# Turning h's columns between the halves of a product, and block 0's order and columns moved, in a routed expert stage

## The chip, the cores and the metric

One core of a Trainium2 chip runs the whole program. The metric is the device time of one execution in microseconds (us). The engines are PE (matrix products; PEld is its weight load, PEldq its sequencer in the rows), DVE, ACT, POOL and SP. DVE and ACT do the arithmetic between products, SP and POOL issue the transfers. Each engine works through its own queue in order, and waits on semaphores of others.

## The reference

Three stages follow each other on 1792 tokens (4 x 448) of 768 features:

```python
attn = 1.0 / (1.0 + np.exp(-(scale * q @ k.T - np.log(S))))    # 12 heads, sigmoid attention
x = attn @ v
do_compute = x @ w_skip > 0                # the other tokens pass unchanged
e_idx = np.argmax(x @ w_gate, axis=1)      # one of 8 experts for each token
y = gate_w * (np.maximum(x @ w1[e], 0.0) @ w2[e])      # w1: 768x1024, w2: 1024x768
x = x + y
g = elu(x @ w_in);  out = g @ w_out        # dense, 768 -> 2048 -> 768
```

All of it is in float32. The kernel makes each product out of three products of split operands (high x high, high x low, low x high), which keeps float32's accuracy.

## The kernel before, in words

**Stages.** Attention with the gate's logits runs until about 205 us of the profiled span, the expert stage until about 465 us, the dense layer to the end. The change is in the expert stage (lines 657 to 1144).

**Blocks.** The tokens that are computed are sorted by expert into blocks of up to 256 slots, two halves of 128 rows. A block has a kind, which PE and the other engines load into a register and branch on (`level`, L1106): SINGLE (first half alone), FEW (second half with at most 64 rows) or WHOLE. With these inputs block 0, 1 and 3 are WHOLE, 2 and 4 are FEW, 5, 6 and 7 are SINGLE, and then `close` (L1067) leads into the dense layer. A block that has two halves passes two branches, L1121 (`few`) and L1125 (`many`); the arm that isn't taken runs `rest` (L1100) instead, which is one tiny instruction on PE, ACT and DVE each. The branch hint ahead of them (`skips`, L1119; it shows as L1367 in the rows) tells PE's sequencer where the branch will go.

**One block.** `columns` (L773) turns the gathered rows into columns: four PE flips per group of features, three groups, into the PSUM tiles pt0, pt1 and acc1 (`ends`); for each group ACT copies the high part (L769) and DVE subtracts for the low part (L771). `hold_up` puts 14 filler products between the first flip of block 0 and the next. Then the products with w1 follow. In WHOLE blocks (`up_two`) h comes out with its features on partitions and needs no turning. In the others (`up_parts`) it comes out by rows; ACT copies it to SBUF (`hs`, L871; `hf`, L873), PE flips it (`h_columns`, L778: half 0 with flips at L138, the second half of a FEW block with L786) and ACT (L793) and DVE (L794) write its high and low columns. `h_columns(0)` turns the first half of h's features, `h_columns(1)` the second. Then `back` (L875) does the products with w2, chunks 4 to 7, each 4 steps of three products in 12 instructions per half (8 for a FEW half): chunks 4 and 5 take the first half of h's features, 6 and 7 the second. `outcome` (L923) adds gate times product into the rows (DVE, L931); for a FEW half ACT first copies y to SBUF (L881) and PE folds it (L930).

**What is left over.** Only chunk 4 of the first half is done inside a block's arm. Chunks 5 to 7 of it run inside the next block, behind that block's `columns` (`between`, L971, and `lead_in`, L985).

**Weights.** SP fetches chunks of 128x1536 into a ring of 13 (L710). For each, ACT casts the high part (L734) and DVE subtracts for the low part (L736), into a ring of 4. `ahead(i, c)` (L820) does that two chunks ahead of use; `ahead(i, 5)` (L902) is the last one in an arm, ahead of `h_columns(1)` on the queues of ACT and DVE.

**Block 0.** `lead_in` (L990) does its columns ahead of the two arms. In its arm the order of tokens and slots for the later gathers is worked out: DVE steps beside the products (`places_in_order`), 12 DVE compares (`order_rows`, L1043), and at the arm's end `slot_order` (L1047): 12 small products into acc1 and a chain of DVE instructions, L1054 to L1065, on which the gather of block 2 waits.

**Order.** PE, ACT and DVE run in the order in which the code is written.

Of the kernel before, what the change touches and what calls it, by code (L numbers as in the profile page):

```python
# [23 lines left out]
P = 128  # L24
# [10 lines left out]
KF1 = F1 // P  # L35
# [6 lines left out]
N2 = DM // 2  # L42
WCH = 1536
FA = 9
TB = 4
NOR = NTT // TB * TB
# [43 lines left out]
def build(nc, tc, a):  # L90
# [3 lines left out]
    with ExitStack() as top:  # L94
# [563 lines left out]
        with ExitStack() as st:  # L658
# [114 lines left out]
            def columns(i):  # L773
                for g in range(3):
                    flip_rows(i, g, ends[g])
                    split_columns(g, ends[g], x2)

            def h_columns(nh, sizes):  # L778
                for h, n in enumerate(sizes):
                    pt = pt_t[(nh + h) % 2].rearrange("p (c n) -> p c n", c=4)[:, :, :n]  # L780
                    for j in range(4):
                        w = slice(j * P, (j + 1) * P)
                        if n == P:
                            flip(pt[:, j, :], hs_t[nh][:, w])
                        else:
                            nc.tensor.matmul(  # L786
                                pt[:, j, :], hf_t[nh][:, w], fold[:, :n], start=True, stop=True
                            )
                    t = slice(h * P, h * P + n)
                    h_hi, h_lo = h2[:, nh, 0, :, t], h2[:, nh, 1, :, t]  # L790
                    if n < P:
                        h_lo = h2[:, nh, 0, :, h * P + n : (h + 1) * P]
                    nc.scalar.activation(h_hi, pt, AF.Relu)  # L793
                    nc.vector.scalar_tensor_tensor(  # L794
                        h_lo, pt, 0.0, h_hi, op0=ALU.max, op1=ALU.subtract
                    )
# [4 lines left out]
            def h_part(s, k):  # L801
                return h2[:, k // 4, s, k % 4]

            def product(o, h, n, a2, i, c, width, k0, total):

                t = slice(h * P, (h + 1) * P)
                for j in range(WCH // width):
                    w = slice(j * width, (j + 1) * width)
                    hi, lo = (u[:, w] for u in weights(i, c))
                    a_hi, a_lo = (a2(s, k0 + j)[:, t] for s in range(2))  # L810
# [61 lines left out]
                        else:  # L872
                            nc.scalar.copy(hf_t[nh], acc_t[(3, 0)[nh]])  # L873

            def back(i, h, n, chunks):  # L875

                for c in chunks:
                    c4, nh = divmod(c - 4, 2)
                    product(py[nh][h], h, n, h_part, i, c, N2, 4 * c4, KF1)
                    if n < P and c4:  # L880
                        nc.scalar.copy(yf_t[nh], py[nh][h])  # L881

            def expert(i, sizes, following=None):
# [5 lines left out]
                        outcome(i - 1, 0, P)  # L889

                if i == 0:
                    split_w(0, 1)
                if whole:
                    up_two(i, aside, soon)
# [8 lines left out]
                if i == 0:  # L903
                    run(aside)
                    order_rows()
                for h, n in list(enumerate(sizes))[1:]:
                    if whole:
                        back(i, h, n, range(4, 8))
                        outcome(i, h, n)
                        back(i, 0, P, range(4, 5))  # L910
                    else:
                        back(i, h, n, range(4, 6))
                        h_columns(1, sizes)
                        back(i, h, n, range(6, 8))
                        back(i, 0, P, range(4, 5))
                        outcome(i, h, n)
                if i == 0:
                    slot_order()
                if len(sizes) == 1:
                    back(i, 0, P, range(4, 5))  # L920
                    h_columns(1, sizes)

            def outcome(i, h, n):  # L923

# [60 lines left out]
            def lead_in(i):  # L985

                if i:
                    back(i - 1, 0, P, range(7, 8))
                else:
                    columns(0)  # L990

            def places_in_order():

# [52 lines left out]

            def slot_order():  # L1047

                og = acc_t[1][:, :NOR]
                for t in range(NOR):  # L1050
                    nc.tensor.matmul(
                        og, one_hot[:, t], ca[:, t], start=(t == 0), stop=(t == NOR - 1)
# [318 lines left out]
```

## Time and profile before

| | us |
|---|---|
| median of 3 timed runs | 950.01 |
| lowest and highest of them | 943.79 and 951.31 |
| the profiled execution | 946.63 |
| its span, first to last instruction | 944.9 |
| PE busy in the span | 907.7 (96%) |

In timeline rows the columns are start (us from the span's start), duration (us), engine, line, operation, output<-inputs, shape and count of merged instructions; the brackets give the engine's idle time just before and what ended it.

### The profile page before, as it was taken

Reading aid. Unit: us, or ns where it says so; the run is one execution under the profiler, and the core shown is the slowest. Engines: PE = TensorE matmul, PEld = TensorE weight load, DVE = VectorE, ACT = ScalarE, POOL = GpSimd, SP = SyncE. Lnnn points to the kernel's source line nnn. Section 1 sums busy time; section 2 is a strip of 40 time slices with the busy share of each in tenths; the row PEclk is TensorE's granted clock in tenths of the full one; section 3 lists DMA queues with packets and bytes.
Section 4 is the critical chain, followed back from the end, with each engine's and each line's share of the span. In section 5 each row is a group of like instructions: output and inputs, shape, how many; then the busy total and the mean of one; then the engine's idle time right before and its main releaser. Section 6 shows DMA issues by size and latency. Waiting matters only on the chain.

```text
span 944.9 us, 13400 instructions
## 1 busy us (share of the span) xinstructions
PE 907.7 (96%) x5047; PEld 738.9 (78%) x5047; DVE 585.7 (62%) x893; ACT 504.5 (53%) x703; POOL 71.2 (8%) x69
## 2 busy tenths in 40 slices
PE   7899999999999899999799999999999999999997
PEld 4555555549998898888688888888888888888997
DVE  4777877967756556688578888533443434434664
ACT  7777776535346336577354455444443444443664
POOL 0000000020220210233100000000000100000100
PEclk9999999999999999999999999999999999999999
DMA  9989897569962583594653333000010100000100
GB/s 247 266 234 272 250 270 246 170 228 404 379 250 84 217 325 115 196 410 185 226 197 101 106 106 107 34 34 1 17 34 18 51 17 1 1 0 1 68 1 34
DMA packets 33989, 139.46 MB, mean 148 GB/s; under 512 B 4874, under 2 KB 5514, under 8 KB 33890
## 3 DMA queue, kind: packets, MB, share of 16 engines
q1 hardware_dynamic: 29410, 119.17, 37.6%
q0 software_dynamic: 4480, 19.01, 5.6%
q8 instruction: 57, 0.93, 0.4%
q14 instruction: 42, 0.34, 0.1%
HBM read 117.58 MB, written 23.60 MB: 149 GB/s over the span
## 4 chain that ended last, share of the span: by engine, by line
PE 82%; DVE 3%; DMA 3%; issue 2%; ACT 2%; SPq 0%; ACTq 0%; DVEq 0%
PE acc L1246 15%; PE pt L1246 9%; PE acc L1213 8%; PE acc L1214 8%; PE acc L1215 8%; PE acc L743 6%; PE acc L745 6%; PE acc L744 6%; PE ps L239 3%; PE po L253 3%; DMA wo<-wo_d 1%; PE acc L815 1%; PE pt L138 1%; PE acc L816 1%; PE acc L138 1%
## 5 line engine op out<-in xcount | busy, mean ns | idle before, releaser
L736 DVE TENSOR_TENSOR wlo<-raw,whi 128x1536 fp32r<-128x1536 f32 x64 | 111.2, 1756 | 35.1 <-ACT whi L734 34.7
L1222 ACT ACTIVATE m<-acc 128x512 f32<-128x512 f32 (+1 forms) x64 | 34.9, 545 | 175.3 <-PE acc L1215 168.6
L1224 DVE SCALAR_TENSOR_TENSOR m<-m,acc 128x512 f32<-128x512 f32 (+1 forms) x64 | 39.7, 621 | 141.9 <-ACT m L1223 141.9
L734 ACT CAST whi<-raw 128x1536 fp32r<-128x1536 f32 x64 | 94.0, 1481 | 25.7 <-DMA raw<-in_w 6.7
L246 ACT ACTIVATE at<-ps,bias 112x896 f32<-112x896 f32 x96 | 89.1, 1008 | 30.4 <-PE ps L239 30.2
L1246 PE MATMUL acc<-wol,gh 128*128 128x256 f32 x320 | 101.0, 316 | 0.0
L1246 PE MATMUL acc<-woh,gl 128*128 128x256 f32 x320 | 100.5, 314 | 0.0
L1246 PE MATMUL acc<-woh,gh 128*128 128x256 f32 x320 | 100.4, 314 | 0.0
L1214 PE MATMUL acc<-x,wih 128*128 128x512 f32 (+1 forms) x270 | 96.0, 356 | 0.0
L1213 PE MATMUL acc<-x,wih 128*128 128x512 f32 (+1 forms) x270 | 95.9, 355 | 0.0
L1215 PE MATMUL acc<-x,wil 128*128 128x512 f32 (+1 forms) x270 | 95.6, 354 | 0.0
L743 PE MATMUL acc<-whi,both 128*128 128x384 f32 (+1 forms) x236 | 84.3, 357 | 0.6 <-PE acc L745 0.6
L744 PE MATMUL acc<-wlo,both 128*128 128x384 f32 (+1 forms) x236 | 83.0, 352 | 0.0
L745 PE MATMUL acc<-whi,both 128*128 128x384 f32 (+1 forms) x236 | 83.0, 352 | 0.0
L253 PE MATMUL po<-at,vt 112*64 112x448 f32 x384 | 77.5, 545 | 0.7 <-DVE xT L261 0.7
L1202 DVE TENSOR_TENSOR wol<-wo,woh 128x768 fp32r<-128x768 f32 x64 | 61.2, 956 | 23.4 <-ACT woh L1201 23.0
L1246 PEld LDWEIGHTS acc<-woh,gh 128*128 128x128 f32 x320 | 60.3, 188 | 10.1
L1246 PEld LDWEIGHTS acc<-wol,gh 128*128 128x128 f32 x320 | 60.3, 188 | 9.3
L1201 ACT CAST woh<-wo 128x768 fp32r<-128x768 f32 x64 | 53.4, 834 | 26.0 <-PE acc L1246 25.9
L1228 DVE TENSOR_TENSOR gl<-m,gh 128x512 fp32r<-128x512 f32 (+1 forms) x64 | 40.0, 626 | 40.5 <-ACT gh L1227 40.5
L1246 PEld LDWEIGHTS acc<-woh,gl 128*128 128x128 f32 x320 | 60.1, 188 | 4.3
L239 PE MATMUL ps<-qs,kh 128*112 128x448 f32 x192 | 58.1, 384 | 3.7 <-ACT at L246 2.2
(234 smaller groups left out, 1950.1 us busy)
## 6 DMA issues: line engine op xcount, KB each, us to landing
raw<-in_w SPq DMA_DIRECT2D x66, 768.0 KB
kr<-in_k SPq DMA_DIRECT2D x22, 448.0 KB
raw<-in_wi SPq DMA_DIRECT2D x9, 768.0 KB
raw<-in_wo SPq DMA_DIRECT2D x9, 768.0 KB
vt<-in_v SPq DMA_DIRECT2D x12, 448.0 KB
x_d<-xr SPq DMA_DIRECT2D x14, 384.0 KB
raw<-in_wi SPq DMA_DIRECT2D x14, 384.0 KB
raw<-in_wo SPq DMA_DIRECT2D x14, 384.0 KB
```

The source lines that it names most:

```text
L239: nc.tensor.matmul(ps[:CP, j, :S], kk[:, 2 * p + j, c * CP : (c + 1) * CP], qs[:, p, j], start=(i == 0), stop=(i == 1),)
L246: nc.scalar.activation(at[:, :, c, :], ps[:CP, :, :S], AF.Sigmoid, bias=bias[:CP], scale=QK_SCALE)
L253: nc.tensor.matmul(po[64 * j : 64 * j + 64, :S], vt[:, 2 * (hp % 2) + j, c, :], at[:, j, c, :], start=(c == 0), stop=(c == NCH - 1),)
L734: nc.scalar.copy(w_hi, raw)
L736: nc.vector.tensor_sub(w_lo, raw, w_hi)
L743: nc.tensor.matmul(o, a_hi, b_hi, start=first, stop=False)
L744: nc.tensor.matmul(o, a_hi, b_lo, start=False, stop=False)
L745: nc.tensor.matmul(o, a_lo, b_hi, start=False, stop=last)
L1213: nc.tensor.matmul(o, a, b, start=(cc == 0), stop=False)
L1214: nc.tensor.matmul(o, a, c, start=False, stop=False)
L1215: nc.tensor.matmul(o, wil[:, cc], b, start=False, stop=(cc == KD - 1))
L1246: nc.tensor.matmul(o, a, b, start=(clears and f == 0 and k_ == 0), stop=(f == KF2 - 1 and k_ == 2), skip_group_check=True,)
```

## The change

Four things change. `h_columns` does the second half (h = 1) first, then half 0. In a FEW arm `h_columns(1)` stands one chunk earlier, between chunks 4 and 5 of h = 1, and `outcome` stands between the two halves (two steps each) of chunk 4 of half 0. In a SINGLE arm `h_columns(1)` stands between those halves and not behind both. In block 0 `slot_order` runs ahead of chunk 4 of half 0 (for a WHOLE block) and writes acc0 instead of acc1, and block 0's `columns` stands in each arm's beginning, so behind the branches.

```diff
             def h_columns(nh, sizes):
-                for h, n in enumerate(sizes):
+                for h, n in reversed(list(enumerate(sizes))):
...
-            def product(o, h, n, a2, i, c, width, k0, total):
+            def product(o, h, n, a2, i, c, width, k0, total, part=slice(None)):
...
-                for j in range(WCH // width):
+                for j in range(WCH // width)[part]:
...
-            def back(i, h, n, chunks):
+            def back(i, h, n, chunks, part=slice(None)):
...
-                    product(py[nh][h], h, n, h_part, i, c, N2, 4 * c4, KF1)
+                    product(py[nh][h], h, n, h_part, i, c, N2, 4 * c4, KF1, part)
...
                 if i == 0:
+                    columns(0)
                     split_w(0, 1)
...
-                for h, n in list(enumerate(sizes))[1:]:
-                    if whole:
-                        back(i, h, n, range(4, 8))
-                        outcome(i, h, n)
-                        back(i, 0, P, range(4, 5))
-                    else:
-                        back(i, h, n, range(4, 6))
-                        h_columns(1, sizes)
-                        back(i, h, n, range(6, 8))
-                        back(i, 0, P, range(4, 5))
-                        outcome(i, h, n)
-                if i == 0:
-                    slot_order()
-                if len(sizes) == 1:
+                start, end = slice(0, 2), slice(2, 4)
+                if whole:
+                    back(i, 1, P, range(4, 8))
+                    outcome(i, 1, P)
+                    if i == 0:
+                        slot_order()
                     back(i, 0, P, range(4, 5))
+                    return
+                if len(sizes) > 1:
+                    back(i, 1, sizes[1], range(4, 5))
                     h_columns(1, sizes)
+                    back(i, 1, sizes[1], range(5, 8))
+                    back(i, 0, P, range(4, 5), start)
+                    outcome(i, 1, sizes[1])
+                    if i == 0:
+                        slot_order()
+                    back(i, 0, P, range(4, 5), end)
+                else:
+                    back(i, 0, P, range(4, 5), start)
+                    if i == 0:
+                        slot_order()
+                    h_columns(1, sizes)
+                    back(i, 0, P, range(4, 5), end)
...
                     back(i - 1, 0, P, range(7, 8))
-                else:
-                    columns(0)
...
-                og = acc_t[1][:, :NOR]
+                og = acc_t[0][:, :NOR]
```

## Rows read from the trace of the kernel before

**Rows 1.** The page, part 4: the chain that ended last, share by engine

```profile
PE 82%; DVE 3%; DMA 3%; issue 2%; ACT 2%; SPq 0%; ACTq 0%; DVEq 0%
```

**Rows 2.** PE's waits in 205 to 475: us in total, times, longest

```profile
PE pt L138 <- DVE both L794: 4.4, 3, 1.5
...
PE acc L815 <- DVE both L794: 1.9, 2, 0.9
PE pt L138 <- issue: 1.9, 1, 1.9
```

**Rows 3.** Timeline of block 0's end, PE first, then DVE

```profile
241.78 0.34 PE L743 MATMUL acc<-whi,both 128*128 128x384 f32 x1
...
243.87 0.46 PE L1051 MATMUL acc<-ca,one_hot 128*128 128x12 f16 x12
244.19 0.64 PE L138 MATMUL pt<-cst,xg 128*128 128x128 f32 x4
246.10 0.33 PE L138 MATMUL pt<-cst,xg 128*128 128x128 f32 x1 [1.28 <-DVE order L1065]
...
241.98 0.62 DVE L931 SCALAR_TENSOR_TENSOR xg<-acc,slot_gate,xg 128x384 f32<-128x384 f32 x1 [0.70 <-PE acc L745]
244.37 0.17 DVE L1054 COPY order_off<-acc 128x12 f32<-128x12 f32 x1 [1.77 <-PE acc L1051]
...
245.88 0.17 DVE L1065 TENSOR_SCALAR order<-order_off 128x12 int32<-128x12 f32 x1
```

**Rows 4.** Timeline of SINGLE block 5's end, ACT and DVE

```profile
405.74 1.49 ACT L734 CAST whi<-raw 128x1536 fp32r<-128x1536 f32 x1
...
407.26 1.76 DVE L736 TENSOR_TENSOR wlo<-raw,whi 128x1536 fp32r<-128x1536 f32 x1 [0.35 <-ACT whi L734]
408.94 0.68 DVE L794 SCALAR_TENSOR_TENSOR both<-pt,both 128x512 fp32r<-128x512 f32 x1
```

**Rows 5.** Timeline of FEW block 4 from its second half of h, by engine

```profile
379.90 1.05 DVE L794 SCALAR_TENSOR_TENSOR both<-pt,both 128x512 fp32r<-128x512 f32 x2
...
388.28 0.15 DVE L1104 COPY rest<-cst 128x1 f32<-128x1 f32 x1
...
384.16 0.48 ACT L881 COPY hf<-acc 128x384 f32<-128x384 f32 x1 [0.92 <-PE acc L816]
...
381.00 0.44 PE L815 MATMUL acc<-whi,both 128*128 128x384 f32 x1 [0.93 <-DVE both L794]
...
388.49 0.33 PE L138 MATMUL pt<-cst,xg 128*128 128x128 f32 x1 [1.01 <-DVE rest L1104]
```

**Rows 6.** Branches and hints of PE's sequencer: ns min/median/max, first and last start

```profile
L1367 PEldq BRANCH_PREFETCH_HINT  x2: 39/40/42, 206.5 to 207.5; - x2
L1121 PEldq COMPARE_BRANCH  x1: 385/385/385, 211.6 to 211.6; - x1
...
L1125 PEldq COMPARE_BRANCH  x2: 438/1900/3361, 313.0 to 313.5; - x2
...
L1367 PEldq BRANCH_PREFETCH_HINT  x1: 35/35/35, 320.7 to 320.7; - x1
L1121 PEldq COMPARE_BRANCH  x1: 891/891/891, 321.9 to 321.9; - x1
...
L1111 PEldq COMPARE_BRANCH  x1: 5783/5783/5783, 462.5 to 462.5; - x1
```

**Rows 7.** Timeline of block 0's beginning, PE, then DVE

```profile
208.29 3.19 PE L761 MATMUL acc<-iota_h 128*128 128x512 f16 x14
...
214.85 0.36 PE L743 MATMUL acc<-both,whi 128*128 128x256 f32 x1 [1.92 <-DVE rest L1104]
215.05 0.28 PE L744 MATMUL acc<-both,whi 128*128 128x256 f32 x1
...
212.76 1.29 DVE L771 TENSOR_TENSOR both<-pt,both 128x512 fp32r<-128x512 f32 x2 [4.05 <-ACT both L769]
```

**Rows 8.** Two stretches: busy PE, PEld, DVE, ACT, POOL (instructions), PEclk, DMA, GB/s

```profile
215.60:219.00 3.40, 3.40 (x19) 3.40 (x18) 1.76 (x1) 1.65 (x2) 0.00 (x0) 0.52 1.01 414
243.00:248.00 5.00, 3.72 (x36) 3.33 (x36) 2.67 (x9) 1.75 (x4) 0.97 (x2) 1.00 1.01 411
```

## The prediction

> **What bounds the kernel now.** I read the chain of waits first: PE carries 82% of it and every other engine 3% or less [rows 1]. So a change pays only where PE stands idle or where its clock is low, and it pays just the idle time that goes. The change touches the expert stage (208 to 470 us). The second view is therefore PE's waits in that stretch, grouped by releaser [rows 2]; the reader is to see that the groups are few and that h's columns (L794, the DVE half of turning h) release PE five times: three times for 1.5 us each in front of the next block's row flips, twice for 0.9 us inside a FEW block. Third, the timeline around each of these waits tells what the releaser itself was queued behind. That is the view that decides here. The other waits (block 0's start and end, the ends of the FEW blocks) are read the same way.
>
> **Single blocks (5, 6, 7): h's columns between the halves of the product.** The three waits are worth 4.4 us together [rows 2], and the change gives each a cover of six products. Twelve of these products run from 241.78 to 243.87 [rows 3], 0.174 us each, so the cover is 1.05 us. I still count nothing, since PE is not what makes L794 late. In block 5, ACT casts the last weights until 407.23, DVE's subtraction for them (L736) runs 407.26 to 409.02, and L794 follows at once, 408.94 to 409.62 [rows 4]. L794 stands behind L736 on DVE's queue in both kernels, because `ahead(i, 5)` is issued ahead of `h_columns(1)` in both. Flipping h 1.05 us sooner lets ACT's relu end sooner, but L794 starts when L736 ends, so PE resumes at the same 409.7. The six products that now follow the flips fill time that PE spent on them before the flips. Cost from both sides: 0, if the queue holds; 3 x 1.05 = 3.2 us gained, if it doesn't. I take 0.
>
> **FEW blocks (2, 4): flips one chunk earlier, second half first.** In block 4 the two L794 start at 379.90 and take 1.05 together, and PE resumes at 381.00 after 0.93 idle [rows 5]. Products and flips only change places in front of that point, so PE arrives at the same time. What changes is which L794 it needs: the products that follow are those of h = 1, whose smaller L794 now goes first. The full-width one takes 0.68 [rows 4], so the small one takes 1.05 - 0.68 = 0.37 and PE resumes near 380.3. The start of the pair doesn't move, as it again stands behind the L736 of `ahead(i, 5)`. Gain 0.7 per block, 1.4 for two; from 0.05 (if the products wait for the pair) to 0.93 each (all the idle time).
>
> **Ends of the FEW blocks: the outcome between the halves.** PE ends block 4 at 388.49 - 1.01 = 387.48 and waits for DVE's `rest` copy (388.28 + 0.15), which stands behind the two gate updates of the outcome [rows 5]. The outcome now comes six products earlier, so `rest` ends at 388.43 - 1.05 = 387.4, and six products lie behind the fold matmuls. PE goes on at about 387.5: gain 1.0. The fold matmuls now have 1.05 us of products, not 2.1, to hide ACT's copy of y behind; the later copy starts at 384.16, released by the last products of h = 1, and takes 0.48 [rows 5], so with the 0.2 until it starts about 0.3 us are to spare. In block 2 the same place has an idle stretch of 1.9 us by "issue" [rows 2], and the branches there show why: one branch of PE's sequencer took 3.361 us [rows 6]. The sequencer comes to it when the fold matmul's semaphore is in, which doesn't move, so I count 0; from -0.3 to +1.9. Together 1.0, from -0.3 to 2.9.
>
> **Block 0's end: the order ahead of the last products.** Today the last twelve products run to 243.87, the 12 small matmuls of the order follow, the flips into pt0 start at 244.19, and those into pt1 wait until DVE has ended its chain L1054 to L1065 (244.37 to 246.05): they start at 246.10 after 1.28 idle [rows 3]. After the change, the small matmuls come first (they need `one_hot` and `ca`, made before the outcome), and the products behind them. PE reaches the pt0 flips at the same 244.19 and the pt1 flips one group later, about 244.6. DVE's chain waits only for the second gate update (242.60): 242.60 + 1.68 = 244.3, in front of 244.6. Gain 246.10 - 244.63 = 1.47, at least 0, at most this. The accumulator moves from acc1, which DVE still reads at 242.60, to acc0, so the order need not wait for it. What stands behind L1065 on other engines comes earlier too: POOL's gather for block 2, needed a whole block later, and DVE's first L771.
>
> **Block 0's start: its columns inside the arm.** Today PE's flips and its own `rest` are over at 212.93, and the first product waits 1.92 us, until 214.85, for DVE's `rest` copy, which stands behind all three subtractions L771 [rows 7]. Inside the arm `rest` runs before the flips, so a product needs only its own group's columns: by the second L771 (212.76 + 1.29 = 214.05) nine products can be done, against about 215.9 now (214.85 and eight steps). That would be 1.7 us. But the arm's branch loses its cover. Its hint is given at 207.5, and the branch comes 4 us later, when the flips are out, and costs 0.385 [rows 6]. In the changed kernel it comes right behind the hint, with the flips behind it. In block 3 the hint is at 320.7 and the branch, begun at 321.9, lasts 0.891: 2.1 us from the hint [rows 6]. By that, PE's sequencer is free at 209.6, the 14 fillers start near 210.0 and not at 208.29 [rows 7], and everything up to L771 shifts by 1.7. The two cancel: 0; from +1.7 (no cost of the branch) to -1.4 (a branch of 3.361: 207.6 + 3.4 + 0.4 is 211.4, a shift of 3.1 less 1.7).
>
> The Trainium skill speaks against this part ("Runtime: NRT & Kernel Launch", section Instruction fetch mechanics: a taken branch to a page that isn't loaded stalls until the page is fetched). The rows of 3.361 and 5.783 us fit it; by the rule alone, with 3.361 as the price, the part loses 1.4 and the sum below is 3.9; by the hinted rows it is even and the sum 5.3.
>
> The clock is the second half of this part. After the flips and the 1.92 us without work the granted clock fell to 0.52 in 215.60 to 219.00, the 1.2 GHz level for nearly all of it [rows 8]: 0.48 x 3.4 = 1.6 us lost. In the changed kernel the idle stretch lies ahead of the fillers (208.2 to 210) and only short waits stand between flips and products; block 0's end, with 1.28 idle between flips, had no such fall (1.00 in 243 to 248). I take it that the clock stays at 2.4 GHz and count 1.4, keeping 0.2 for a branch a little slower; from 0 to 1.6.
>
> **Sum.** 0 + 1.4 + 1.0 + 1.5 + 1.4 = 5.3 us. Nothing between block 1 and the dense stage gives it back: PE has no wait on a weight or a gather there [rows 2]. The profiled execution took 946.63 us (944.9 of span, 1.7 around it): 941.3. The three timed runs have their median 3.4 us above it and spread over 7.5 us; I set the base at the middle of the two, 948.3, and forecast 943.0. A measurement of this kernel can tell about 1% (9.5 us) from no change, so this is a gain that will hardly be told.
>
> **Rivals.**
> (a) Slower: the branch at block 0's start. At the end of the stage, at 462.5, a branch took 5.783 us [rows 6]. If the one at 207.6 takes that, the fillers start at 207.6 + 5.8 + 0.4 = 213.8, 5.5 us late; less the 1.7 of finer waits that is 3.8, and the clock stays low for longer than now by as much again (1.6), so that the 1.4 is not gained. Then 1.4 + 1.0 + 1.5 - 3.8 - 1.6 = -1.5: 949.8, slower than the base. It decides from a branch of about 4.3 us on. Against it: hinted branches took at most 2.1 from their hint.
> (b) The arm's branch takes 3.361 (1.4 less), and half of the FEW terms (1.2) stay behind DVE's queue: 5.3 - 1.4 - 1.2 = 2.7, so 945.6. For it: one branch in the rows took that long, and every L794 stands behind an L736. Against it: that branch had no hint close ahead. (The first half of this is the Trainium skill's rule from above.)
> (c) The single blocks gain as well: 3.2 more, 939.8. For it: PE's wait does name L794. Against it: DVE's row of L736 ends where L794 starts.
> (d) All of it is lost at the dense stage's start, where PE waits for a branch and for loads: 948.3, no change. Against it: that branch begins when PE's last wait is over, and so moves along.
> Code moves too: each arm of block 0 gets its own flips, so page borders shift against all later branches. A stall such as block 2's can go, or come elsewhere; 1 to 2 us either way, in the range of each case.
>
> **How the numbers follow.** Forecast 0.55, (a) 0.08, (b) 0.2, (c) 0.1, (d) 0.07. The range 938.0 to 950.0 holds (b), (c), (d) and (a) at its edges, and the spread of the runs. Faster by over 1% would need (c) and luck with the runs: 0.11. Slower by over 1% would need more than (a): 0.03. Within 1%: 0.86.
>
> **What would show it.** Right: in the single blocks the 1.5 us wait for L794 in front of the pt1 flips is still there, with L736 right ahead of L794; in the FEW blocks the wait is 0.2 to 0.3; the wait at block 4's end is gone; block 0's second flip group starts 0.4 after the first; the first arm branch lasts about 2 us, and the clock in the 3 us behind the first products is full. Wrong: a single block whose flips run without a wait; a branch over 4 us; a clock at 0.5 in block 0; or a PE wait for weights in blocks 1 to 7.

## The result, and the profile after

| | before | after |
|---|---|---|
| median of 14 runs (us) | 946.38 (943.79 to 951.31) | 952.49 (947.24 to 956.46) |
| profiled execution: time, span (us) | 946.63, 944.9 | 952.29, 950.5 |
| mean granted clock | 0.993 | 0.987 |

The ratio is 1.0054, 95% interval 1.0041 to 1.0068. The change makes the kernel slower by half a per cent; I had forecast 943.0. Both profiled executions lie near their medians, so their traces can be compared stage by stage.

I cut both PE timelines at the first matmul behind each block's first branch (from block 1 on, the first row flip). What lies between is the time of a block, in us; the other rows are experiments told of below.

```
                 blk 0  blk 1  blk 2  blk 3  blk 4  blk 5  blk 6  blk 7    sum
before           36.00  36.82  36.38  35.46  35.64  19.13  20.63  21.40  241.46
after            34.62  35.24  33.56  41.10  33.62  27.03  20.67  20.62  246.46
b_pad26          36.79  36.78  35.32  39.26  35.50  23.05  20.66  20.66  248.02
b_cols           34.08  36.78  35.50  38.35  35.25  26.05  20.63  20.63  247.27
e1_lead          36.24  35.24  35.21  35.31  33.58  20.68  20.68  20.66  237.60
e1_noend         35.75  35.24  35.32  35.31  34.75  19.13  20.65  20.77  236.92
b_end            36.02  36.82  36.19  35.73  34.58  20.55  20.63  20.83  241.35
a_nocopy         35.16  35.24  35.26  35.84  33.69  26.21  20.63  20.67  242.70
a_nocopy_hint    35.23  35.24  35.17  35.12  33.58  19.11  20.68  20.66  234.79
```

Five blocks became 8.6 us shorter together (1.4 + 1.6 + 2.8 + 2.0 + 0.8). Two became 13.5 us longer: block 3 by 5.6 and block 5 by 7.9. The difference lies in these two; all that lies outside the eight blocks adds 0.7.

PE's waits from 205 to 475 us, grouped by releaser (us in total, times, longest), in the kernel after:

```profile
PE pt L138 <- DVE both L794: 4.4, 3, 1.5
PE acc L743 <- issue: 4.0, 1, 4.0
...
PE acc L1108 <- issue: 2.7, 1, 2.7
PE acc L745 <- issue: 2.2, 1, 2.2
PE pt L138 <- DVE rest L1110: 1.3, 1, 1.3
```

Against [rows 2] the reader sees three things. The single blocks' 4.4 us stand unchanged. The two waits of 0.9 for L794 in the FEW blocks are gone, and so is the 1.9 us stretch by "issue" at block 2's end. In their place stand three new stretches by "issue", 8.9 us together: time for which the profile shows no releaser. So the next view is PE's sequencer, its branches as in [rows 6] (ns min/median/max, first and last start). Two of them matter: `few`, which leads a block with two halves into its arm, and `two` (L1118 in the kernel before), which tells such a block from a SINGLE one, whose arm I call the one-group arm:

```profile
L1127 PEldq COMPARE_BRANCH  x1: 5932/5932/5932, 316.3 to 316.3; - x1
```

```profile
L1124 PEldq COMPARE_BRANCH  x1: 5969/5969/5969, 390.1 to 390.1; - x1
```

The first is `few` of block 3, which took 0.891 before [rows 6]. The second is `two` of block 5; before, the same branch reads:

```profile
L1118 PEldq COMPARE_BRANCH  x1: 435/435/435, 392.3 to 392.3; - x1
```

The idle time is not the whole price. Stretches of the kernel after (busy time of PE, PEld, DVE, ACT, POOL with instructions, then PEclk, DMA share, GB/s):

```profile
319.50:322.30 2.80, 0.13 (x2) 0.04 (x1) 0.00 (x0) 0.00 (x0) 2.19 (x3) 0.86 1.01 412
...
324.00:326.00 2.00, 2.00 (x11) 2.00 (x11) 1.96 (x2) 1.38 (x2) 0.00 (x0) 0.50 1.05 420
326.00:328.00 2.00, 2.00 (x11) 2.00 (x11) 2.00 (x3) 0.00 (x0) 0.00 (x0) 0.50 0.98 353
```

```profile
392.00:396.20 4.20, 0.21 (x3) 0.03 (x1) 3.83 (x3) 1.47 (x1) 2.06 (x2) 1.00 1.03 421
396.20:399.00 2.80, 2.80 (x10) 2.80 (x11) 0.00 (x0) 0.00 (x0) 1.33 (x2) 0.57 1.01 419
399.00:402.00 3.00, 0.84 (x4) 0.56 (x3) 0.00 (x0) 0.00 (x0) 0.00 (x0) 0.83 1.00 374
```

In this execution PE's granted clock is low for a while after both branch stalls: 0.50, the 1.2 GHz level, from 322.3 to about 328, and again at the start of block 5's products. Block 3: 2.67 idle plus half of some 6 us is 5.7, against 5.6 measured. Block 5: 3.99 and 2.16 idle, plus 0.43 x 2.8 for the clock and half of the 0.7 us that PE still worked before its second stall, is 7.7 of the 7.9 lost. That accounts for both blocks.

### The profile page after: what moved, and what is told of

Same layout as the page of the kernel before. It is cut to its first block, busy times and chain, and to the rows that moved or that the text cites. A ratio compares the mean times of both kernels' runs of the same rounds, so it can differ in the third digit from the quotient of the medians.

```text
span 950.5 us, 13407 instructions
## 1 busy us (share of the span) xinstructions
PE 913.0 (96%) x5047; PEld 741.1 (78%) x5047; DVE 585.8 (62%) x893; ACT 504.3 (53%) x703; POOL 66.4 (7%) x69
## 4 chain that ended last, share of the span: by engine, by line
PE 82%; DVE 3%; issue 2%; ACT 2%; DMA 1%; SPq 0%; DVEq 0%; ACTq 0%
PE acc L1252 15%; PE pt L1252 9%; PE acc L1219 8%; PE acc L1220 8%; PE acc L1221 8%; PE acc L743 6%; PE acc L744 6%; PE acc L745 6%; PE ps L239 4%; PE po L253 3%; PE acc L138 1%; PE pt L138 1%; PE acc L815 1%; PE acc L816 1%; DMA raw<-in_wi 1%
## 5 line engine op out<-in xcount | busy, mean ns | idle before, releaser
L736 DVE TENSOR_TENSOR wlo<-raw,whi 128x1536 fp32r<-128x1536 f32 x64 | 111.2, 1755 | 34.4 <-ACT whi L734 33.7
L743 PE MATMUL acc<-whi,both 128*128 128x384 f32 (+1 forms) x236 | 85.8, 364 | 4.0 <-issue 4.0
L745 PE MATMUL acc<-whi,both 128*128 128x384 f32 (+1 forms) x236 | 83.5, 354 | 2.2 <-issue 2.2
L1252 PEld LDWEIGHTS acc<-woh,gh 128*128 128x128 f32 x320 | 60.3, 188 | 10.1
L1202 DVE TENSOR_TENSOR wil<-wi,wih 128x768 fp32r<-128x768 f32 x60 | 57.4, 956 | 6.7 <-ACT wih L1201 6.0
```

The source lines that it names most:

```text
L736: nc.vector.tensor_sub(w_lo, raw, w_hi)
L743: nc.tensor.matmul(o, a_hi, b_hi, start=first, stop=False)
L745: nc.tensor.matmul(o, a_lo, b_hi, start=False, stop=last)
L1252: nc.tensor.matmul(o, a, b, start=(clears and f == 0 and k_ == 0), stop=(f == KF2 - 1 and k_ == 2), skip_group_check=True,)
```

## The experiments

Three theories. P (T1 in the first four expectations) and T2 were mine before the first run, D came out of the first four:

- **P, the place of the code.** Block 0's columns now stand in each of its arms. The FEW arm of block 0 isn't taken with these inputs, but its copy lies in the program: 12 flips and 14 fillers, each a weight load and a matmul, 52 instructions. All later code moves by so much against the 16 KB pieces in which code is fetched (queue 8 of the DMA view: 56 packets, 0.92 MB in the kernel after).
- **D, the page comes late.** The FEW blocks' outcome now comes earlier, so the transfers behind it start earlier, and block 5's page of code, asked for by the hint, has to come through them.
- **T2, the new order itself** makes the stalls, wherever the code lies.

All ratios are to the kernel before on the same chip, with 95% intervals.

| kernel | ratio | block 3's branch (us) | block 5's branch (us) |
|---|---|---|---|
| before | 1 | 0.89 | 0.44 |
| after | 1.0054 (1.0041 to 1.0068) | 5.93 | 5.97 |
| e1_lead | 0.9985 (0.9972 to 0.9998) | 0.73 | 3.23 |
| b_pad26 | 1.0074 (1.0048 to 1.0101) | 5.87 | 0.45 |
| a_pad102 | 1.0057 (1.0034 to 1.0081) | 0.73 | 6.29 |
| b_cols | 1.0076 (1.0056 to 1.0096) | 5.94 | 2.24 |
| a_else102 | 1.0005 (0.9987 to 1.0024) | 1.21 | 3.18 |
| e1_noend | 0.9933 (0.9910 to 0.9956) | 0.35 | 0.46 |
| e1_ahead | 1.0004 (0.9985 to 1.0022) | 0.84 | 5.96 |
| e1_else80 | 1.0115 (1.0081 to 1.0149) | 2.52 | 5.98 |
| b_end | 1.0022 (0.9996 to 1.0048) | 1.15 | 3.10 |
| a_noend | 1.0063 (1.0043 to 1.0083) | 6.11 | 1.48 |
| noend_split | 0.9990 (0.9975 to 1.0005) | under 0.6 | 0.84 |
| noend_pad10 | 0.9952 (0.9933 to 0.9970) | under 0.6 | under 0.6 |
| a_nocopy | 0.9987 (0.9961 to 1.0012) | 1.04 | 6.09 |
| a_nocopy_noend | 0.9958 (0.9940 to 0.9977) | under 0.6 | 1.15 |
| b_end_hint | 0.9993 (0.9981 to 1.0006) | 0.66 | 0.36 |
| e1_hint | 0.9950 (0.9931 to 0.9970) | 0.83 | 0.36 |
| a_nocopy_hint | 0.9945 (0.9921 to 0.9970) | under 0.6 | under 0.6 |

The branches, and the block times above, are those of one profiled execution of each kernel. That execution took 4 to 5 us more than the median in a_else102, e1_ahead, a_nocopy and noend_pad10 (954.28, 952.41, 951.2 and 947.37), so their stalls need not be those of the median.

**Is it the place of the code? e1_lead, b_pad26, b_cols, a_pad102.**

```diff
# e1_lead: after, block 0's columns back in lead_in
                 if i == 0:
-                    columns(0)
                     split_w(0, 1)
...
                     back(i - 1, 0, P, range(7, 8))
+                else:
+                    columns(0)
```

> The changed kernel with one part undone: block 0's columns stand in lead_in again, so the arms of block 0 hold no second copy of them and every later block's code lies within a few instructions of where it lay before the change; the other parts (FEW order, block 0's end) stay. T1 (code position): the steps keep their gain (about 1.5 at block 0's end, 1.4 to 2.4 in the FEW blocks), the branches of 5.9 us of blocks 3 and 5 and the 2.2 us stall are gone: 942 to 945, ratio to before 0.995 to 0.999. T2 (the new order and its timing make the stalls): two branches near 5.9 us stay in blocks 3 and 5: 950 to 953, ratio 1.004 to 1.007.

944.85. Block 3's stall is gone; the gains of blocks 1 and 4 stay, and 1.2 of block 2's 2.8. Block 5's branch is shorter, but at 3.23 it isn't gone: a first sign that one cause is not enough.

```diff
# b_pad26: before, code that never runs in block 0's FEW arm
+            def unused(n):
+
+                for _ in range(n):
+                    nc.tensor.matmul(acc_t[5][:, :2], iota_h, iota_h[:, :2], start=True, stop=True)
...
                             expert(i, (P, FEW))
+                            if i == 0:
+                                unused(26)
```

> The kernel before with 26 never-executed matmuls added to block 0's FEW arm, which isn't taken with these inputs: nothing that runs changes, all code behind lies 52 instructions later, as much as the second copy of block 0's columns moves it in the changed kernel. T1: stalls come where after has them, blocks 3 and 5 (two branches of 5 to 6 us): 6 to 9 us slower than before, 952 to 955, ratio 1.006 to 1.010. T2: no change, ratio 0.999 to 1.001, no new branch over 3 us.

953.69. Not one instruction that runs differs from before, and block 3's branch is that of the kernel after:

```profile
L1126 PEldq COMPARE_BRANCH  x1: 5869/5869/5869, 322.1 to 322.1; - x1
```

For block 3, T2 falls here. Block 5's branch stays at 0.45, though the block is 3.9 longer, for another stall, among its products:

```profile
402.35 0.39 PE L743 MATMUL acc<-whi,both 128*128 128x512 f32 x1 [2.23 <-ACT whi L734]
```

That is the counterpart of the 2.16 us by "issue" that after shows at much the same point of the block. The cast named here had ended at 401.68, 0.67 earlier, and a piece of code landed at 400.95, 1.4 before PE went on. The stalls of this kind in b_cols (3.5 us) and a_noend (3.0) ended 1.4 and 1.2 after a piece too. So I take the code to be what was late (the branch lands 52 instructions nearer to the end of its piece than in before, so the border comes sooner); that is inferred from these intervals, and no run tests it. The shift alone costs 6.6 us of the stage (248.02 against 241.46).

```diff
# b_cols: before, only block 0's columns moved into the arms
                 if i == 0:
+                    columns(0)
                     split_w(0, 1)
...
-                else:
-                    columns(0)
```

> The kernel before with block 0's columns moved into the arms alone, nothing else of the change. T1: code lies 52 instructions later, so stalls in blocks 3 and 5 as in the changed kernel, without the gains of the FEW blocks and of block 0's end: 953 to 956, ratio 1.007 to 1.010. T2 (the new order of the FEW blocks and of block 0's end makes the stalls): no stalls there, block 0's start even or 1 to 2 us better by the clock: 944 to 947, ratio 0.998 to 1.000.

954.05, as P has it: 5.94 in block 3, and a stretch of 3.5 us by "issue" in block 5's products. Block 5's branch took 2.24 although the outcome is late here, so the early outcome isn't the only thing that lengthens it. Block 0 itself is 1.9 shorter than before: the step does what it was meant to do, and costs 7.7 in the other blocks, four times as much.

a_pad102 puts 102 never-executed matmuls in the same FEW arm of the kernel after, so that with the copy 256 instructions are added, which the expectation counts as one piece of 16 KB.

> The changed kernel with 102 never-executed matmuls (204 instructions) in block 0's FEW arm: with the 52 of the columns' copy that makes 256 instructions, 16 KB, so that the code of blocks 1 to 7 lies on the same offsets within 16 KB as before the change. T1 (offset within a 16 KB page decides): stalls of blocks 3 and 5 gone, all gains kept: 940 to 943, ratio 0.993 to 0.997. T2: as the changed kernel, 950 to 953, ratio 1.004 to 1.007.

952.9, a miss for the total and a hit for the place: block 3's branch is at 0.73, as P has it. But the longer arm made the branch across it at block 0's start take 7.0 us:

```profile
L1132 PEldq COMPARE_BRANCH  x1: 7004/7004/7004, 208.1 to 208.1; - x1
```

and block 5's branch stayed at 6.29. Block 3 follows the place; block 5's branch doesn't come back with it.

**What makes block 5's branch long? a_else102, e1_noend, b_end, a_noend.**

a_else102 has the 102 matmuls in block 0's one-group arm, behind block 0's own code (the same lines, ahead of that arm's lead_in).

> The changed kernel whole, with 102 never-executed matmuls in block 0's one-group arm (not taken, and behind block 0's own code): blocks 1 to 7 lie on the offsets within 16 KB that they had before the change, block 0 lies as in the changed kernel. P (place of the code): block 0's first branch takes 0.5 as in the changed kernel and not the 7.0 of a_pad102, block 3's arm branch under 1 and not 5.9, block 2's end about 3.0 again. D (page late at block 5, because the early outcome starts the weight loads earlier): block 5's branch stays at 3 to 6.3. Both: 943 to 946, ratio 0.996 to 1.000. If the new order itself makes block 3's stall: 950 to 953, ratio 1.004 to 1.007.

948.96, above the 943 to 946 expected. Block 0's first branch no longer stalls, block 2's end has its 3.4 again, block 3's is 1.2, block 5's 3.2: both theories hold where they apply. The pad made the jump at block 0's end longer, and that branch now took 5.87 in the profile (block 0 is 40.8 long), which I take to be why the total missed.

```diff
# e1_noend: e1_lead, the FEW blocks' outcome behind all products again
-                    back(i, 0, P, range(4, 5), start)
+                    back(i, 0, P, range(4, 5))
                     outcome(i, 1, sizes[1])
                     if i == 0:
                         slot_order()
-                    back(i, 0, P, range(4, 5), end)
```

> The changed kernel with block 0's columns in lead_in and with the FEW blocks' outcome behind all products again (the flips one chunk earlier stay). D: the weight loads behind block 4 start later again, the page of block 5's arm is there, its branch takes about 0.4 (3.2 with the early outcome) and PE's 1.3 us in front of block 5's products go; the wait of 1.0 at block 4's end comes back: 943.5 to 945.5, even with the kernel of columns in lead_in (944.85). Rival (the branch is late by its place, whatever the outcome's place): 3.2 stays and 1.0 comes on top: 946 to 947, ratio 0.999 to 1.001.

942.23, the lowest ratio of all. Block 5's branch is at 0.457, block 5 takes its old 19.13, block 4 gives up 1.2. That is as D has it. The median is 2.6 us below e1_lead's where I had expected a draw; in the profiles the stage is only 0.7 shorter (236.92 against 237.60).

b_end is the same test from the other side, and the cleanest:

```diff
# b_end: before, with the outcome between the halves in the FEW blocks
-                        back(i, 0, P, range(4, 5))
+                        back(i, 0, P, range(4, 5), slice(0, 2))
                         outcome(i, h, n)
+                        back(i, 0, P, range(4, 5), slice(2, 4))
```

> The kernel before with one edit: in the FEW blocks the outcome stands between the halves of the last product. The program has as many instructions for PE as before, so no code moves to another place. D (the early outcome makes block 5's page late): block 4's end loses its wait of 1.0, but block 5's branch takes 3 to 6 (0.435 before) and PE idles 1.3 to 4 behind it: 947 to 953, ratio 1.000 to 1.006. Prediction's step alone (only the wait goes): 946, ratio 0.999, branch 0.4.

947.24. Outside the FEW arms no code changed its place, and block 5's branch went from 0.435 to 3.1 (the total, 1.0022 with 1 inside its interval, would not tell):

```profile
L1119 PEldq COMPARE_BRANCH  x1: 3102/3102/3102, 392.2 to 392.2; - x1
```

Block 4 is 1.06 shorter, the 1.0 that I had predicted, and block 5 is 1.42 longer. The transfers show why. The 6.4 us from the hint on, in 40 slices of 0.16 us (busy share of the DMA engines in tenths), before and then b_end:

```profile
DMA  4000000000000000001004889597993956989978
```

```profile
DMA  5000000000010009999494799799696976997989
```

Before, the engines are all but idle for 3.5 us after the hint (22 slices), but for the first piece of code; with the outcome early the weight loads fill them from 2.4 us on (slice 15). And in the first 5 us after the hint, queue 8, which brings PE's code, landed this many pieces, before and then in b_end (packets, MB, share):

```profile
q8 instruction: 2, 0.03, 3.0%
```

```profile
q8 instruction: 1, 0.02, 1.6%
```

Before, the second piece comes ahead of the loads; in b_end it hasn't come after 5 us, and the branch, 5.3 us after the hint, has to wait for it. The piece landed 7.1 us after the hint (393.99) where before had it at 4.7 (390.57). That the branch itself comes 1.1 us sooner after the hint is the smaller part. In the kernel after the loads begin 2.2 us after the hint (slice 14):

```profile
DMA  4000000000000099818997899892957956979979
```

a_noend takes the early outcome out of the kernel after, by the edit of e1_noend.

> The changed kernel whole, but for the FEW blocks' outcome, which stands behind all products again. P and D together: block 3's branch of 5.9 stays (its place is that of the changed kernel), block 5's falls from 6.0 to about 0.4, the 2.2 us stall in its products goes too: 952.3 less 6 to 8 plus 1: 945.5 to 948.5, ratio 0.998 to 1.001. If the place alone decides in both blocks: 952 to 954, ratio 1.005 to 1.007. If the outcome's place decides in both: 940 to 942, ratio 0.992 to 0.994.

952.43, no gain: a miss for the total. Its profile has block 3's 6.11 (place) and block 5's branch down from 5.97 to 1.48, as P and D have it, with block 5 at 22.3 instead of 27.0. But 1.9 of it goes back in blocks 2 and 4, the stall among block 5's products grew to 3.0, and in this execution the clock was at 0.67 in block 0's fillers (214 to 218), so block 0 took 36.8. Which of these holds in the other runs, one profile doesn't tell.

**A hint given earlier: b_end_hint, e1_hint.** If the piece is asked for too late, asking sooner must help:

```diff
# both: in the FEW arm, behind the last products of h = 1
+                    if i + 1 < NB:
+                        skips(f"two{i + 1}", following >> 1)
...
-                            expert(i, (P, FEW))
+                            expert(i, (P, FEW), following)
```

> The kernel before with the outcome between the halves in the FEW blocks (b_end), and in the FEW arm the hint for the next block's first arm branch given already behind its last products of h = 1, some 4 us earlier than now (26 more instructions in the program, 2 in each block). D: the page is there, block 5's branch falls from 3.1 to about 0.45, PE's 1.2 idle behind it goes: 945 to 946, ratio 0.998 to 0.9995. Rival (the time since the hint doesn't matter): 3.1 stays, 947.

> The changed kernel with columns in lead_in (e1_lead) and the same earlier hint. D: block 5's branch falls from 3.2 to about 0.45, so that the early outcome keeps its 1.0: 941 to 943, ratio 0.992 to 0.995. Rival: as e1_lead, 944.9, ratio 0.9985. Block 2's branch may change too, since its arm now gives a hint for block 3.

946.44 and 941.84. In b_end_hint block 5's branch falls from 3.1 to

```profile
L1121 PEldq COMPARE_BRANCH  x1: 358/358/358, 389.2 to 389.2; - x1
```

with the outcome as early as in b_end, block 4 at 34.58 and block 5 at 19.13. In e1_hint it is 0.364. D is shown from both sides: the early outcome makes the stall, and an earlier request takes it away. In the medians the request tells in e1_hint (0.9950 against e1_lead's 0.9985, intervals just apart), and not in b_end_hint, whose interval overlaps b_end's.

**The place without any pad: a_nocopy, a_nocopy_noend, a_nocopy_hint.** Pads lengthen jumps, so the copy itself was taken out.

```diff
# a_nocopy: after, no columns in block 0's FEW arm (not taken here)
                 if i == 0:
-                    columns(0)
+                    if len(sizes) == 1 or whole:
+                        columns(0)
                     split_w(0, 1)
```

> The changed kernel without the columns in block 0's FEW arm, which isn't taken here (so that arm would be incomplete if it ran); nothing that runs changes, the code of all blocks from 1 on lies 52 instructions earlier, within 5 of where columns in lead_in put it. P: block 3's branch falls from 5.9 to about 0.8, block 2's rises from 0.2 to about 3, block 0 keeps its 34.6 us, block 5 keeps a branch of 3 to 6 (early outcome): 943.5 to 946, ratio 0.996 to 0.999. If the copy isn't the cause: 952, ratio 1.005.

946.45. Block 3's branch is back at

```profile
L1128 PEldq COMPARE_BRANCH  x1: 1035/1035/1035, 321.2 to 321.2; - x1
```

block 2's is at 3.1, block 5's stays at 6.09, and block 0 keeps 0.8 of its gain. For block 3, P holds without a pad.

> The same, and the FEW blocks' outcome behind all products again: both causes gone, columns in the arms, h's columns between halves, block 0's order ahead of its last products. P and D: block 3's branch about 0.4 to 0.8, block 5's about 0.4; against columns in lead_in (e1_noend, 942.2) block 0 gains the clock's 1.4 as predicted: 940 to 942, ratio 0.991 to 0.994. If columns in the arm don't pay: 942 to 944.

942.72: as expected against before, though block 5's branch took 1.15 where 0.4 was expected. Against e1_noend's ratio (0.9933) its 0.9958 is no gain; the intervals overlap, so whether the columns in the arm pay in the median is not settled, though block 0 is 0.8 shorter in the profile.

> The changed kernel with all its steps, without the columns in block 0's FEW arm (not taken here, the arm would be incomplete if it ran) and with the earlier hint for the next block's first branch: block 3's branch about 0.8, block 5's about 0.4. If the steps are worth what was predicted (5.3): 941 to 942, ratio 0.993 to 0.996, with block 0 about 1.2 shorter than in before, block 1 1.6, block 2 0.7 to 1.1, block 4 2.0. If they are worth less together: 943 or more.

941.73, a ratio of 0.9945. All four steps of the change are in it, and neither stall. The stage takes 234.79, 6.7 less than before. From the kernel after to here the stage lost 3.8 us with the copy (a_nocopy, 242.70) and 7.9 more with the hint; in the medians it was about 6.3 and 4.0. So how the cost divides between the two causes is settled only roughly.

**The single blocks: e1_ahead, noend_split.** Is L794 late because L736 is ahead of it on DVE?

```diff
# e1_ahead: e1_lead; noend_split moves only the lo half (DVE)
-                ahead(i, 5)
+                if i == 0 or len(sizes) > 1:
+                    ahead(i, 5)
...
                     h_columns(1, sizes)
+                    if i:
+                        ahead(i, 5)
```

> The changed kernel with block 0's columns in lead_in, and in the one-group arm the casts of the next weights moved behind h's second columns, so that on DVE L794 no longer stands behind the weights' subtraction L736 (blocks 5 to 7). Theory of the prediction (L736 ahead on DVE's queue makes L794 late): the waits of 1.5 in front of the next block's flips fall to 0.5 or less, 3 us faster than with the casts ahead: 941 to 942.5, ratio 0.994 to 0.996. Rival (another step makes L794 late, or the casts become late instead): wait of 1.5 stays or moves to a weight: 944 to 946, ratio 0.998 to 1.000.

> The kernel with columns in lead_in and the outcome behind all products (e1_noend), and in the one-group arm of blocks 5 to 7 the second half of the last weight split (L736, DVE) behind h's second columns; its first half (the cast on ACT) stays ahead. Theory of the prediction (L794 is late because L736 is ahead of it on DVE): the three waits of 1.5 fall to 0.5 or less, 939 to 940.5 where e1_noend took 942.2, ratio 0.990 to 0.992. Rival (L736 is then late for the next block's beginning, as in e1_ahead): 942 or more. The code is 25 instructions longer, so a branch can cost 1 to 5 more or less.

948.45 and 945.14, both slower than the expectations that rest on the theory. The waits of noend_split, from 205 to 475 us:

```profile
PE acc L138 <- DVE wlo L736: 3.3, 3, 1.1
...
PE pt L138 <- DVE both L794: 0.9, 3, 0.3
```

The wait for L794 fell from 4.4 to 0.9, so the reason that I gave is right. But the next thing late is L736 itself, 3.3 us in the flips behind it. Blocks 5 and 7 take 19.04 and 20.73 against e1_noend's 19.13 and 20.77: nothing is left of it. (Block 6 had a branch of 4.1 in this execution.) In e1_ahead, where the cast goes along, L736 costs two waits of 1.9, and block 5's branch was at 5.96.

**Other places: e1_else80, noend_pad10.**

> The changed kernel with block 0's columns in lead_in and 80 never-executed matmuls (160 instructions, 0.62 of 16 KB) in block 0's one-group arm, which isn't taken: another place for the code of blocks 1 to 7, nothing that runs changes. P: the stalls at block 2's end (2.9) and at block 3's arm (0.7) change in size, either both small (942 to 943, ratio 0.995) or one near 6 (946 to 950); a place with both small shows that the change's gain is there without a stall. If the place doesn't matter: 944.9 again, with 2.9 and 0.7.

959.94, slower than either theory had allowed: block 1's branch took 5.4, block 3's 2.5, block 5's 6.0, block 6's 3.8. Here the place changed the branches of four blocks, and I can't foretell from it which branch will stall.

> e1_noend with 10 never-executed matmuls (20 instructions) in block 0's FEW arm, not taken. P: block 2's arm ends 20 instructions further behind a 16 KB border than now (4 behind it), so that the next page is asked for earlier: the branch of 3.1 at block 2's end falls below 1.5, 1 to 1.5 us faster than e1_noend: 940.5 to 941.5, unless block 3's branch grows to 5.9 as with 52 instructions: 946. Place without effect: 942.2.

942.82. Block 2's branch took 3.1 as ever: 20 instructions were not enough to change it, and my reading of the border there fell. So the rule that ties place to stall stays open.

## Why the prediction was wrong

Step by step, by the block times and waits above:

**Single blocks, 0.** Right: 4.4 us in the same three waits, and noend_split shows L736 to be the reason. What I gave as the upper bound, 3.2 if the queue doesn't hold, was wrong: without the queue the next wait takes 3.3.

**FEW blocks and their ends, 1.4 + 1.0.** Right in mechanism, a little low. PE resumes in block 4 at 380.07 after the first L794 alone, and the fold matmuls run into the next products without a wait:

```profile
386.39 0.18 PE L1108 MATMUL acc<-iota_h 128*128 128x2 f16 x1
386.43 1.07 PE L138 MATMUL pt<-cst,xg 128*128 128x128 f32 x8
```

where [rows 5] had 1.01 idle. Block 4 gained 2.0 against 1.7. Block 2 gained 2.8, since its branch of 3.361 went as well; the copy's shift took that one (b_pad26 has block 2 at 35.32 by the shift alone, 1.06 less). That gain isn't one of the step: with the code where it was (e1_lead) block 2 gains 1.2.

**Block 0's end, 1.5.** Right: 1.58 in block 1, in after and in all experiments of the table of blocks that have the step. The order's chain on DVE ends before the last products do:

```profile
242.62 0.17 DVE L1071 TENSOR_SCALAR order<-order_off 128x12 int32<-128x12 f32 x1
```

and eight flips follow at 242.90 without a stop, where [rows 3] had 1.28 idle.

**Block 0's start, 0 + 1.4.** The size is right, 1.38, the way to it only in part. The branch took 0.482 and was over at 208.14, where I had PE's sequencer free at 209.6. What held PE back was DVE's `rest` copy (209.46 to 209.61), behind the subtraction L736 for the first weights (207.79 to 209.54), which I hadn't looked for. That the fillers start at 209.84, near the 210.0 that I had said, is luck. The clock part came as forecast: the clock in the 3 us behind the first products is full where [rows 8] had 0.52:

```profile
209.71 0.30 PE L138 MATMUL pt<-cst,xg 128*128 128x128 f32 x1 [1.26 <-DVE rest L1110]
209.84 3.19 PE L761 MATMUL acc<-iota_h 128*128 128x512 f16 x14
```

```profile
214.60:218.00 3.40, 3.20 (x25) 3.01 (x26) 2.93 (x4) 3.15 (x3) 0.00 (x0) 1.00 1.02 422
```

But it isn't so in every execution: a_noend has the same code in block 0, and there the clock was at 0.67 in 214 to 218.

**Block 7, not in the sum.** Its 0.8 is the branch into its arm: 1.97 in the kernel before (at 432.7), 0.45 after. That branch had its hint at 426.8, 6 us ahead, so the row also speaks against what I wrote under rival (a), that hinted branches took at most 2.1 from their hint: this one ended 7.9 after it.

**The step that failed first: "Code moves too ... 1 to 2 us either way".** I had seen that code moves and that a stall can come elsewhere, and priced it by the stall that might go (1.9 idle), within each case. The measured price of the move is 6.6 us of the stage (b_pad26): a branch of 5.9 in block 3, a stall of 2.2 in block 5, and the low clock behind each, which that term did not count. The clock in b_pad26 behind block 3's stall and then behind block 5's:

```profile
327.00:331.00 4.00, 2.93 (x14) 2.88 (x15) 1.25 (x1) 2.76 (x2) 1.30 (x2) 0.67 1.01 416
331.00:335.00 4.00, 4.00 (x34) 4.00 (x33) 3.23 (x4) 0.09 (x1) 0.00 (x0) 0.90 1.02 379
...
402.50:406.00 3.50, 3.50 (x11) 2.78 (x11) 1.73 (x2) 0.48 (x1) 3.02 (x2) 0.64 1.02 423
406.00:409.00 3.00, 3.00 (x12) 2.35 (x11) 1.76 (x1) 1.71 (x3) 0.39 (x1) 0.85 1.02 403
```

The row for it was there: 5.783 at the dense start [rows 6]. I used it for rival (a), at block 0's start, the one place where the new code gets a branch, and not at the places to which old code moves. Rival (a) so had the right price at the wrong place. What I had as either a stall that goes or one that comes is both at once: in all 19 profiles, where block 2's last branch takes 2.9 to 3.4 us, block 3's takes 0.3 to 1.2, and where it takes 0.2 (after, b_pad26, b_cols, a_noend, e1_else80), block 3's takes 2.5 to 6.1.

**The step that failed second: "Nothing between block 1 and the dense stage gives it back".** I looked for a weight or a gather that would be late. What became late was PE's own code for block 5: the outcome that ends block 4 six products sooner starts the loads some 1.1 to 1.3 us sooner after the hint (slice 15 or 14 for 22), ahead of the piece. The 1.0 won there cost 1.4 in b_end, and with the shift on top 7.9 in the kernel after.

**The base.** I set it at 948.3, between the profiled execution and three runs; the median of 14 is 946.4. The profiled execution was the better guide.

The sum of the steps held: with both stalls away (a_nocopy_hint) the ratio is 0.9945, 5.2 us of 948, where I had 5.3. That it fits to 0.1 is luck: the interval is 2.8 to 7.5 us, and the 6.7 of the profile hold 0.7 from block 7's branch and 0.3 from block 3, which are no steps of mine, with only 0.8 of the 1.4 in block 0. The range failed because the cost of moved code was put at 1 to 2 us when rows of 3.361 and 5.783 stood in the profile.

The Trainium skill's rule that I weighed ("Runtime: NRT & Kernel Launch", section Instruction fetch mechanics: a taken branch to a page that isn't loaded stalls until the page is fetched) agrees with the long branches here, 2.2 to 7.0 us. The same section holds the crossing of a page border in straight code to be mostly hidden; here a stall of 2.16 us by "issue" among block 5's products ended at 401.88, 1.3 after a piece had landed (400.60), soon after a branch into the piece before it. If that is such a crossing, it wasn't hidden, and the measurement decides.

What stays open: by which rule the place makes a branch stall. 52 instructions more cure block 2's branch (0.2 for 3.361) and spoil block 3's; 20 change neither. Nor is it known why block 5's branch takes 3.1 to 3.2 us in three of the kernels with the early outcome and the old hint (b_end, e1_lead, a_else102) and about 6 in four (after, a_nocopy, a_pad102, e1_ahead). It was not tried whether an earlier hint cures block 3's branch in the kernel after, as it cured block 5's in three others (b_end_hint, e1_hint, a_nocopy_hint).

The two best kernels with all their arms complete are e1_noend (0.9933) and e1_hint (0.9950). Their intervals overlap, so which is better isn't settled.

## What to carry to other kernels

Where PE's program has branches, code that never runs still has a price: before code is copied into an arm, ask what lies behind it, and price a stall at the longest branch in the rows plus the low clock that may follow it. When a step frees a buffer or an engine earlier, list what it lets start, the loads above all, and what else must come through the same queues just then, code included. A hint for a branch belongs ahead of the burst of loads, not between it and the branch.

## What the runs showed that I had not expected

- Code comes over the 16 DMA engines that bring the weights, and block 5's piece of it races the loads. With the first packet of the loads 3.5 to 3.6 us after the hint its branch took 0.4 to 1.2 us (six kernels), with 3.3 us 1.5 and 2.2 (a_noend, b_cols, both with the late outcome), with 2.2 to 2.6 us 3.1 to 6.3 (seven kernels). The kernels with a second hint and e1_else80, whose block 4 ends in a stall of its own, are not in this count. A second hint, given 10.1 us ahead of the branch (379.2 for 389.2) where the other stands 5.2 ahead, turned 3.1 us into 0.36.
- Each long branch that I followed ended 1.35 to 1.42 us after a 16 KB piece had landed on queue 8: at 315.55 for 316.90 (block 2 of before), 320.86 for 322.21 and 394.69 for 396.11 (blocks 3 and 5 of after).
- Never-executed instructions, 52 of them, cost 0.74% of the kernel's time (1.0048 to 1.0101), and 160 of them, in e1_else80, took the ratio from 0.9985 to 1.0115.
- The low clock behind a stall is not a fixed price. Block 3's stall was 2.6 to 2.7 us long in three kernels: in after some 6 us at 1.2 GHz followed (0.50 from 322.3 to 328), which more than doubled its price, in b_pad26 less (0.67 and 0.90 in the windows above), in b_cols none (1.00 from 328 to 336). The block took 41.1, 39.3 and 38.4.
